# Linear attention and a gated mixing layer: two token tiles of batch 0 in plain float32, a second buffer for weight combinations, shorter roots

## The chip, the cores and the metric

One core of a Trainium2 chip runs the whole program. The metric is the device time of one execution in microseconds; a version's time is the median of its runs. TensorE multiplies matrices, VectorE, ScalarE (called ACT in the rows) and GpSimd (called POOL) do the elementwise work, and SyncE (SP) issues nearly all transfers. Each engine takes its instructions strictly in the order in which the program lists them, and waits on semaphores for what the others produce.

## The reference

Batch 4, 4 heads, 1088 tokens, head width 32 (together 128 columns), hidden width 1024.

```python
phi(x): a = S1 x; b = S2 x (8 numbers each); phi = outer(a, b)      # 64 features a token
kv = sum_s phi(k) v^T;  z = sum_s phi(k)
x  = phi(q) kv / (phi(q) z + 1e-6)                                   # heads side by side: x is [b, 1088, 128]
h  = gelu_tanh(x @ w_in);  u, v = halves of h                        # 512 columns each
v  = (v - mean(v)) / sqrt(var(v) + 1e-6) * g_ln                      # over the 512 columns
v_s[b, t, d] = sum_s w_sg[t, s] v[b, s, d] + b_sg[t]                 # mixing over the tokens
out = x + (u * v_s) @ w_out
```

`w_in`, `w_out`, S1 and S2 arrive as 64-bit floats and are taken apart on the chip; the rest is float32.

## The kernel before, in words

**Arithmetic.** A product of float32 operands is made of three products in the faster format `float32r`: each operand is rounded to a high word (a cast on ScalarE) and a remainder (the operand minus its high word, a subtraction on VectorE or GpSimd), and high x high, remainder x high and high x remainder are added up in PSUM. So the weights of the mixing stand in SBUF as `w_h` (high words, step `whi`, line 668) and `w_l` (remainders), and the normalised values as `ar` (both words). A few small products (features, attention) are plain float32 products; in the trace such a product stands as two records, a `float32r` product as one.

**Tiles.** The 1088 tokens are nine tiles of 128 (the last of 64). The mixing of one batch is cut into four blocks `db` of 128 hidden columns and, along the output tokens, three pieces `CH` of 420, 420 and 248. For batch 0, blocks 0 and 1 are made in the plain way: for each token tile t and piece, `z0` (block 0, line 690, into `po`) and the loop at line 1249 (block 1, into `pz` and one `ps` buffer) issue the high and remainder products of the values with `w_h` first, and the products with `w_l` later (`low`). All later batches use sums and differences of weight blocks, which save products.

**The start.** Batch 0's attention comes first: `first_loads` (line 434) brings S, k, q, v, `w_in` and the raw weight tiles `w_f` (544 KB each) in; `k1_0`, `features`, `k2_0` and `kv_0` make kv, `q2_0`, `qa`, `qp` and `q3_0` the numerator and denominator, `xd_0`, `xt_0`, `tr_0`, `x1` and `x2` make x (high `x_h`, low `x_l`), piece by piece (three pieces). Then, tile by tile, `v1_0` projects (three products), the gelu runs on ScalarE, VectorE takes mean and variance (`stats_0`, tiles 0 to 5) or ScalarE the sums (tiles 6 to 8), and the reciprocal root follows in groups of tiles, `GROUPS0` = (0,1), (2..5), (6..8): `Gate.first` makes the variance and a first guess from its bits (three small VectorE steps), `Gate.rest` (nine VectorE steps, group 0) or `Gate.rest_g` (11 or 12 GpSimd steps, groups 2 and 6) the root. A tile is scaled (`v3`, VectorE at line 666 or ScalarE at line 333), and `part` (line 670) makes its two words for the products.

**Remainders of the weights.** GpSimd makes them for tiles 0 to 6, three pieces each (`w_lo`, line 708, 21 steps), VectorE for tiles 7 and 8 (`late_low`, line 714). The pool `w` has ten buffers of a tile: nine raw tiles and one free; a remainder takes the buffer of the raw tile that the one before it has finished with, and the last buffer left becomes `t4a`. `HOLD` puts a copy into GpSimd's order so that a root is not delayed by remainders.

**Combinations.** `combine` (line 879) makes the sums and differences of the weight blocks for the later batches in eight rounds (four tile pairs, two halves of 210 columns). A round loads three pieces of the raw weights from DRAM into `tmp` (lines 891, 893), adds and subtracts on VectorE (lines 896 to 899), casts on ScalarE (lines 901, 902), makes remainders (903, 904) and stores high words and remainders to `td` in DRAM (line 906). All eight rounds use the one `tmp`: four parts for the sums and their remainders and three parts for the high words. `stream` brings the stored blocks back later. Beside it, `attention(1)` prepares batch 1 (k features at line 267, `q` products at line 976, its projections at lines 1037 to 1039, gelu 1046, squares 1049).

**The order of work.** A planner object only records steps with their dependencies; the order is written out by hand in `ORDER`, a list of all 1839 step numbers. A program walks it and issues each step on its engine, so each engine's queue is the list cut down to its steps. Some VectorE and GpSimd steps are marked `port`: a marked GpSimd step waits for the marked VectorE step listed before it.

Of the kernel before, what the change touches and what calls it, by code (L numbers as in the profile page):

```python
# [18 lines left out]
P = 128  # L19
# [13 lines left out]

LOWS = 7
ONA = ("wi1", "wi0", "wo")
HOLD = {12:0,15:2}
V30 = "VAVAVAAAA"
STAT = "VVA"
NORM = "VGG"
# [98 lines left out]
def f32(ap):  # L138
    return ap.bitcast(F32)
# [66 lines left out]
def tile_kernel(ctx: ExitStack, tc: tile.TileContext, qd, kd, vd, sd, wd, bd, wind, gd, woutd, identd, outd):  # L206
# [54 lines left out]
    for i in range(WARM):  # L261
        mm(pst[i % 3][:64, :64], lhsT=kp0[:, :64], rhs=kp0[:, :64], start=True, stop=True)

    def features(out, a, b):

        sh = [P, 2, 2, R, R]
        return V.tensor_tensor(  # L267
# [157 lines left out]
    for t in range(NT):  # L425
        w_f[t] = wpool([P, S], "w", f"w_f{t}")
# [952 lines left out]
```

## Time and profile before

| | |
|---|---|
| median of 3 runs | 323.56 us (322.67 to 324.0) |
| the profiled execution's own time | 325.58 us |
| its span, first to last instruction | 323.5 us |
| granted TensorE clock, mean | 0.999 of 2.4 GHz |
| busy: TensorE, VectorE, ScalarE, GpSimd | 310.4, 255.2, 206.7, 48.6 us |
| first mixing product | 33.09 us |

Times in the rows count from the first instruction. A row of an engine's order of time gives the start, the duration, the engine, the line, output and inputs, the shape and the count; brackets give the idle time before it and what ended it. Products overlap each other in the array, so a product lasts longer in its record than the step to the next one; the step is what it costs. The chain of waits is followed back from the last instruction: each piece is what the next one waited for.

### The profile page before, as it was taken

To read this page: it belongs to the slowest core of one execution; us is meant where nothing else is said; L and a number is where in the kernel's file an instruction comes from. 1 tells how busy PE (TensorE), PEld (TensorE's weight loads), DVE (VectorE), ACT (ScalarE), POOL (GpSimd) and SP (SyncE) were. 2 spreads that over 40 slices of the span, in tenths; PEclk is the share of its full clock that TensorE was granted. 3 is DMA by queue.
4 is the path that set the end of the run, shared out by engine and by line. 5 is a ranking of instruction groups with operands and counts; after the bars stand their busy time and mean duration, and the time that the engine had idled before them with its cause. 6 is when DMAs were issued, how large, how long until landed. Compare 5 with 4: busy or idle time off the path is not lost.

```text
span 323.5 us, 6439 instructions
## 1 busy us (share of the span) xinstructions
PE 310.4 (96%) x2318; PEld 282.2 (87%) x2318; DVE 255.2 (79%) x561; ACT 206.7 (64%) x491; POOL 48.6 (15%) x126
## 2 busy tenths in 40 slices
PE   7897999999998799999999999999999999999995
PEld 5565998998887798898899998988899999999995
DVE  4888989999957799987894497989874686878765
ACT  5589973738969886456877864528899933234321
POOL 0396791000003200000050200000006000000000
PEclk9999999999999999999999999999999999999999
DMA  6997775655876757678389047832173049005802
GB/s 203 369 305 265 238 199 175 201 164 158 249 209 191 203 173 220 146 247 239 98 261 321 6 131 246 265 88 63 28 266 135 1 113 305 34 21 165 283 6 69
DMA packets 42126, 57.08 MB, mean 176 GB/s; under 512 B 4080, under 2 KB 37104, under 8 KB 42096
## 3 DMA queue, kind: packets, MB, share of 16 engines
q1 hardware_dynamic: 41952, 56.64, 57.2%
q8 instruction: 18, 0.29, 0.4%
q14 instruction: 12, 0.10, 0.1%
q10 hardware_dynamic: 144, 0.05, 0.1%
HBM read 46.73 MB, written 9.95 MB: 175 GB/s over the span
## 4 chain that ended last, share of the span: by engine, by line
PE 70%; DMA 12%; DVE 7%; ACT 4%; SPq 3%; issue 2%; POOL 1%; DVEq 0%; ACTq 0%; POOLq 0%
PE pz L843 14%; PE pz L845 14%; PE pz L844 14%; DMA td<-tmp 3%; PE ps L758 2%; DMA tmp<-in_w 2%; PE ps L760 2%; PE ps L759 2%; PE pz L854 2%; DMA r<-in_q 2%; PE pz L855 2%; PE po L795 2%; DMA td<-w_l 2%; PE po L796 2%; PE po L797 2%
## 5 line engine op out<-in xcount | busy, mean ns | idle before, releaser
L843 PE MATMUL pz<-w_h,ar 128*128 128x420 f32 (+1 forms) x288 | 94.0, 327 | 0.0
L845 PE MATMUL pz<-w_l,ar 128*128 128x420 f32 (+1 forms) x288 | 93.1, 323 | 0.5 <-DMA w_l<-td 0.5
L844 PE MATMUL pz<-w_h,ar 128*128 128x420 f32 (+1 forms) x288 | 93.2, 324 | 0.0
L843 PEld LDWEIGHTS pz<-w_h,ar 128*128 128x128 f32 x288 | 54.1, 188 | 5.0 <-issue 1.8
L845 PEld LDWEIGHTS pz<-w_l,ar 128*128 128x128 f32 x288 | 54.2, 188 | 1.6 <-DMA w_l<-td 0.9
L844 PEld LDWEIGHTS pz<-w_h,ar 128*128 128x128 f32 x288 | 54.1, 188 | 1.0
L818 ACT CAST ar<-vn 128x512 fp32r<-128x512 f32 x40 | 24.7, 619 | 23.7 <-PE pz L845 18.2
L789 ACT CAST gh<-gt 128x420 fp32r<-128x420 f32 (+1 forms) x47 | 22.9, 493 | 24.1 <-DVE gt L788 22.1
L764 ACT ACTIVATE u<-ps 128x420 f32<-128x420 f32 (+1 forms) x48 | 22.0, 468 | 12.2 <-PE ps L760 10.7
L790 DVE TENSOR_TENSOR gl<-gt,gh 128x420 fp32r<-128x420 f32 (+1 forms) x47 | 24.9, 534 | 6.0 <-ACT gh L789 5.8
L819 DVE TENSOR_TENSOR ar<-vn,ar 128x512 fp32r<-128x512 f32 x40 | 27.1, 683 | 2.1 <-ACT ar L818 1.8
L333 ACT ACTIVATE vn<-vn,st 128x512 f32<-128x512 f32 x33 | 25.6, 812 | 0.9 <-POOL st L327 0.8
L788 DVE TENSOR_TENSOR gt<-gt,u 128x420 f32<-128x420 f32 (+1 forms) x47 | 24.8, 534 | 1.3 <-ACT u L764 0.4
L712 POOL TENSOR_TENSOR w_l<-w_f,w_h 128x420 fp32r<-128x420 f32 (+1 forms) x21 | 21.4, 1045 | 14.4 <-DVE sp_wi_t L492 12.7
L1049 ACT ACTIVATE kp<-vn,st 128x512 bf16<-128x512 f32 x27 | 19.4, 720 | 3.3 <-DVE vn L267 2.9
L774 DVE SCALAR_TENSOR_TENSOR gt<-pz,g_col,b_bc 128x420 f32<-128x420 f32 (+1 forms) x31 | 17.5, 571 | 3.9 <-PE pz L845 2.2
L1046 ACT ACTIVATE vn<-ps 128x512 f32<-128x512 f32 x27 | 16.0, 593 | 4.9 <-PE ps L1039 4.8
L316 POOL TENSOR_TENSOR st<-st 128x4 f32<-128x4 f32 (+2 forms) x8 | 2.1, 268 | 100.6 <-DVE st L298 100.6
L758 PE MATMUL ps<-x_h,win_h 128*128 128x420 f32 (+1 forms) x48 | 16.2, 337 | 0.1
L759 PE MATMUL ps<-x_h,win_l 128*128 128x420 f32 (+1 forms) x48 | 15.7, 328 | 0.0
L760 PE MATMUL ps<-x_l,win_h 128*128 128x420 f32 (+1 forms) x48 | 15.7, 327 | 0.0
L795 PE MATMUL po<-gh,wout_h 128*128 128x420 f32 (+1 forms) x47 | 15.7, 333 | 0.0
(260 smaller groups left out, 703.1 us busy)
## 6 DMA issues: line engine op xcount, KB each, us to landing
w_h<-td SPq DMA_DIRECT2D x26, 420.0 KB
w_l<-td SPq DMA_DIRECT2D x52, 210.0 KB
td<-tmp SPq DMA_DIRECT2D x16, 315.0 KB
w_f<-in_w SPq DMA_DIRECT2D x9, 544.0 KB
eb<-dq SPq DMA_DIRECT2D x6, 364.0 KB
ea<-dq SPq DMA_DIRECT2D x12, 182.0 KB
vn<-in_k SPq DMA_DIRECT2D x3, 576.0 KB
tmp<-in_w SPq DMA_DIRECT2D x8, 210.0 KB
```

The costliest lines, as they stand in the source:

```text
L333: return A.activation(self.vn(t), self.vn(t), AF.Identity, bias=self.nm[:, t : t + 1], scale=self.rs[:, t : t + 1])
L758: mm(o, lhsT=win_h[:, ws], rhs=xh[:, cs], start=True, stop=False)
L759: mm(o, lhsT=win_l[:, ws], rhs=xh[:, cs], start=False, stop=False)
L760: mm(o, lhsT=win_h[:, ws], rhs=xl[:, cs], start=False, stop=True)
L788: add("V", dv(cw), lambda: V.tensor_mul(gt(k)[:, :cw], gt(k)[:, :cw], utt[plan.got[u]][:, :cw]), r=[u], w=[k], free=[u], port=1)
L789: add("A", ac(cw), lambda: A.copy(ght[plan.got[h]][:, :cw], gt(k)[:, :cw]), r=[k], take={h: "gh"})
L790: add("V", dv(cw), lambda: V.tensor_sub(glt[plan.got[l]][:, :cw], gt(k)[:, :cw], f32(ght[plan.got[h]][:, :cw])), r=[h, k], take={l: "gl"}, ...
L818: add("A", ac(n), lambda: A.copy(dst[:, 0], q()), r=r, w=[key])
L819: add("V", dv(n), lambda: V.tensor_sub(dst[:, 1], q(), f32(dst[:, 0])), r=r, w=[key], port=1)
L843: mm(o, lhsT=ar[e][:, 0, t], rhs=wh, start=first, stop=False, skip_group_check=True)
L844: mm(o, lhsT=ar[e][:, 1, t], rhs=wh, start=False, stop=False, skip_group_check=True)
L845: mm(o, lhsT=ar[e][:, 0, t], rhs=wl, start=False, stop=last, skip_group_check=True)
```

## The change

- **`WHOLE = (0, 1)`**: in blocks 0 and 1 of batch 0, token tiles 0 and 1 are multiplied in one plain float32 product each, the scaled values `vn` with the raw weights `w_f`. Their `part` steps and their products with words are gone. Their remainders `w_l`, which later batches need, are made by VectorE after the last raw product (`late_low`, put behind `raws`); GpSimd makes all remainders of tiles 2 to 8. The pool's buffers are handed out in the order 2 to 8, 0, 1.
- **`tm2`**: the second half of each combination round has a buffer of its own for the four parts; the high words (`hi`) stay in the one `tmp`.
- **Roots**: `first` is two steps, not three; it runs on GpSimd wherever `rest_g` follows. `rest` is eight steps, not nine: a polynomial in place of two rounds of Newton's method.
- The split of S gives two of its eight steps to ScalarE; the split of `w_in`'s second half gives one subtraction (`l1`) to GpSimd. The switches `KG`, `QG` and `FILL` are empty or zero: their new branches run nothing.
- **`ORDER`** is a new list of 1816 steps. SyncE now loads: S, the large piece of k, the small piece of k, q's first third, v (two), `w_in`'s second half, q's other thirds, the identity, `w_f` 2, 3, a piece of batch 1's q, `w_f` 4, `w_in`'s first half, a piece of batch 1's q, the first pieces of `tmp`, batch 1's k, then `w_f` 0, 1, 8, 6, 5, 7. Before it was: S, the small piece of k, q's first third, `w_in`'s second half, the large piece of k, v's first part, q's second third, v's second part, `w_f` 0, the identity, q's last third, `w_f` 1, 2, 3, batch 1's k. VectorE's list now has, after the last statistics: the root of tiles 0 and 1, the scaling of tile 0, one combination step, and only then the first features of batch 1. TensorE's list has the projections in the tile order 2, 3, 4, 0, 5, 1, 6, 7, 8, then two q products and three k products of batch 1, then ten of the twelve raw products before the first product of tile 2's words; batch 1's key-value products come later. GpSimd's list has eight remainder pieces, then the roots of groups 2 and 6, then the other thirteen pieces.

```diff
+ROOT = (1.0, 0.99999624, 1.49998809, 2.51218104, 4.40140684)
+WHOLE = (0, 1)
 LOWS = 7
-ONA = ("wi1", "wi0", "wo")
-HOLD = {12:0,15:2}
+ONA = ("s", "wi1", "wi0", "wo")
+HOLD = {}
+LOWG = ("wi1",)
...
+    tm2 = const([P, 4 * HW], "tm2")
...
-        def first(self, t0, n, summed=True):
+        def first(self, t0, n, summed=True, by=None):
             ve, y = (x[:, :n] for x in self.ch[t0][:2])
...
-            V.tensor_scalar(yi, ve.bitcast(I32), 1, None, op0=ALU.logical_shift_right)
-            return V.tensor_scalar(yi, yi, -1.0, float(0x9EF759DF), op0=ALU.mult, op1=ALU.add)
+            return by.tensor_scalar(y.bitcast(I32), ve.bitcast(I32), -0.5, float(0x1EF759DF), op0=ALU.mult, op1=ALU.add)
...
             V.tensor_mul(h, y, y)
             V.tensor_mul(h, h, ve)
-            V.tensor_scalar(p, h, 1.5, 2.5, op0=ALU.mult, op1=ALU.add)
-            V.tensor_mul(p, p, h)
-            V.scalar_tensor_tensor(y, p, 1.875, y, op0=ALU.add, op1=ALU.mult)
-            V.tensor_mul(h, y, y)
-            V.tensor_mul(h, h, ve)
-            V.scalar_tensor_tensor(self.rs[:, ts], h, 1.5, y, op0=ALU.add, op1=ALU.mult)
+            V.tensor_scalar(h, h, 0.5, None, op0=ALU.add)
+            V.scalar_tensor_tensor(p, h, ROOT[3] / ROOT[4], h, op0=ALU.add, op1=ALU.mult)
+            for c in ROOT[2:0:-1]:
+                V.scalar_tensor_tensor(p, p, c / ROOT[4], h, op0=ALU.add, op1=ALU.mult)
+            V.scalar_tensor_tensor(self.rs[:, ts], p, ROOT[0] / ROOT[4], y, op0=ALU.add, op1=ALU.mult)
...
-    for t in range(NT):
+    turns = [t for t in range(NT) if t not in WHOLE] + list(WHOLE)
+    for t in turns:
         w_f[t] = wpool([P, S], "w", f"w_f{t}")
...
-        onA = n > 16 and name in ONA
+        onA = name in ONA
...
-            step(("first", t0), "V", 0.49, lambda t0=t0, n=n, s=summed: g.first(t0, n, s), bn, port=1)
-            step(("norm", t0), "G", 4.1, lambda t0=t0, n=n, s=summed: g.rest_g(t0, n, s), [("first", t0)])
+            step(("norm", t0), "G", 4.1, lambda t0=t0, n=n, s=summed: (g.first(t0, n, s, G), g.rest_g(t0, n, s))[1], bn)
...
+        if t in WHOLE:
+            mm(o, lhsT=vn[:, t, :P], rhs=w_f[t][:, c0 : c0 + cw], start=t == 0, stop=False, skip_group_check=True)
+            return
...
-                s = tmp[:, : 4 * HW].rearrange("p (a c) -> p a c", c=HW)
+                s = (tm2 if h else tmp)[:, : 4 * HW].rearrange("p (a c) -> p a c", c=HW)
                 hi = f32r(tmp[:, 4 * HW :].rearrange("p (a c) -> p a c", c=HW))
-                k = [("tmp", i) for i in range(4)]
+                k = [("tm2" if h else "tmp", i) for i in range(4)]
...
-            add("V", 0.55, lambda t0=t0, n=n: g.first(t0, n), r=mk, w=[nk], port=1)
-            add("G", 3.5, lambda t0=t0, n=n: g.rest_g(t0, n), r=mk, w=[nk])
+            add("G", 3.9, lambda t0=t0, n=n: (g.first(t0, n, by=G), g.rest_g(t0, n))[1], r=mk, w=[nk])
...
+                if t in WHOLE:
+                    mm(o, lhsT=vn[:, t, P : 2 * P], rhs=w_f[t][:, cs], start=t == 0, stop=False, skip_group_check=True)
+                    return
...
         if i == NT - 1:
+            for t in WHOLE:
+                lo = late_low(t, lo + raws)
             for x in range(NT):
-                for cj in range(3):
+                for cj in range(3 if x not in WHOLE else 0):
```

## Rows read from the trace of the kernel before

**Rows 1.** The page's parts 1 and 2: busy us by engine; traffic in 40 slices of 8.09 us.
```profile
PE 310.4 (96%) x2318; PEld 282.2 (87%) x2318; DVE 255.2 (79%) x561; ACT 206.7 (64%) x491; POOL 48.6 (15%) x126
...
GB/s 203 369 305 265 238 199 175 201 164 158 249 209 191 203 173 220 146 247 239 98 261 321 6 131 246 265 88 63 28 266 135 1 113 305 34 21 165 283 6 69
```

**Rows 2.** Stretches: us, busy us (count) of PE, PEld, DVE, ACT, POOL, clock, DMA share, GB/s.
```profile
27.88:33.09 5.21, 3.01 (x69) 2.60 (x68) 4.61 (x21) 5.11 (x20) 3.25 (x14) 1.00 0.64 214
...
94.00:110.00 16.00, 13.52 (x159) 11.85 (x158) 11.56 (x31) 12.84 (x37) 2.47 (x11) 1.00 0.71 216
...
160.00:314.20 154.20, 154.20 (x1052) 145.37 (x1051) 114.83 (x239) 90.92 (x214) 12.21 (x44) 1.00 0.47 146
```

**Rows 3.** TensorE in order of time: start, us, line, shape, count.
```profile
20.12 0.50 PE L633 MATMUL ps<-win_h,x_h 128*128 128x512 f32 x1
...
27.49 0.40 PE L635 MATMUL ps<-win_h,x_l 128*128 128x512 f32 x1
...
33.09 0.38 PE L697 MATMUL po<-w_h,ar 128*128 128x248 f32 x1
...
34.05 0.35 PE L697 MATMUL po<-w_h,ar 128*128 128x420 f32 x1
34.24 0.35 PE L699 MATMUL po<-w_h,ar 128*128 128x420 f32 x1
```

**Rows 4.** VectorE in order of time, 22 to 33 us.
```profile
22.07 0.70 DVE L639 BATCH_NORM_STATS2 st<-vn 128x6 f32<-128x512 f32 x1 [0.59 <-ACT vn L650]
...
28.63 0.17 DVE L296 TENSOR_SCALAR st<-st 128x2 f32<-128x2 f32 x1
...
31.00 1.09 DVE L267 TENSOR_TENSOR vn<-ps,kb 128x256 f32<-128x256 f32 x3
32.01 0.54 DVE L666 TENSOR_SCALAR vn<-vn,st 128x512 f32<-128x512 f32 x1
```

**Rows 5.** TensorE in order of time, its two waits between 94 and 110 us.
```profile
98.28 1.15 PE L941 MATMUL ps<-sk,vn 128*64 128x64 f32 x24 [0.81 <-ACT vn L1046]
...
108.55 0.53 PE L976 MATMUL ps<-qld,sk 128*64 128x180 f32 x4 [1.66 <-ACT u L764]
```

**Rows 6.** The chain of waits, 98 to 106 us: start, us, what.
```profile
98.52 2.70 DMA td<-tmp
101.24 4.08 DMA tmp<-in_w
```

**Rows 7.** ScalarE in order of time, the cast of line 901.
```profile
106.66 0.72 ACT L901 CAST tmp<-tmp 128x630 fp32r<-128x630 f32 x1 [1.56 <-DVE tmp L898]
```

**Rows 8.** The queue of SyncE, two of the first loads.
```profile
2.10 0.43 SPq L444 DMA_DIRECT2D sg_wraw_wi<-in_w_in  x1
2.58 0.43 SPq L437 DMA_DIRECT2D k<-in_k  x1
```

**Rows 9.** TensorE in order of time, 9 to 11.3 us.
```profile
9.04 0.92 PE L526 MATMUL ps<-sk,k 128*64 128x64 f32 x24 [1.48 <-DMA k<-in_k]
10.37 0.56 PE L604 MATMUL ps<-r,sg_sab 64*128 64x384 f32 x1 [0.41 <-DMA r<-in_q]
...
10.77 0.48 PE L604 MATMUL ps<-r,sg_sab 64*128 64x384 f32 x1
...
11.22 2.32 PE L534 MATMUL pz<-sg_vx,vn 128*64 128x64 f32 x72
```

**Rows 10.** The chain of waits, plain float32 products in batch 0 and at the end.
```profile
11.29 2.25 PE pz L534 x72
...
319.39 0.55 PE po L1200 x2
...
320.35 0.47 PE po L1200 x2
```

**Rows 11.** GpSimd's groups by line and shape: count, busy us, mean ns.
```profile
L712 POOL TENSOR_TENSOR w_l<-w_f,w_h 128x420 fp32r<-128x420 f32 x14 | 16.2, 1174 | 12.8 <-DVE sp_wi_t L492 12.7
L712 POOL TENSOR_TENSOR w_l<-w_f,w_h 128x248 fp32r<-128x248 f32 x7 | 5.5, 787 | 1.6 <-DVE st L298 1.6
```

More of the change, by code (lines that the diff above doesn't have):

```diff
@@ L262, in tile_kernel, with features @@
         mm(pst[i % 3][:64, :64], lhsT=kp0[:, :64], rhs=kp0[:, :64], start=True, stop=True)
[L264 removed]
+    def features(out, a, b, by=None):
         sh = [P, 2, 2, R, R]
[L267 removed]
+        return (by or V).tensor_tensor(
             out.rearrange("t (p h i j) -> t p h i j", p=2, h=2, i=R),
[L269 removed]
+            (a.rearrange("t (p h i) -> t p h i", p=2, h=2) if by else a[:, :64].rearrange("t (p x h i) -> t p x h i", p=2, x=2, h=2)[:, :, 0]).unsqueeze(4).broadcast_to(sh),
             b.rearrange("t (p h j) -> t p h j", p=2, h=2).unsqueeze(3).broadcast_to(sh),
@@ L666, in tile_kernel @@
                 step(("v3", t), "V", 0.45, lambda t=t: V.tensor_scalar(g.vn(t), g.vn(t), g.rs[:, t : t + 1], g.nm[:, t : t + 1], op0=ALU.mult, op1=ALU.add), [("norm", t0)], w=vk[t], port=1)
+    for i in range(FILL):
+        k = ("fill", i)
+        if i < FILL // 2:
+            step(k, "PE", 0.2, lambda k=k: (mm(ps(k)[:64, :64], lhsT=sk[:, :64], rhs=sk[:, :64], start=True, stop=True),
+                                            mm(ps(k)[:64, :64], lhsT=sk[:, :64], rhs=sk[:, :64], start=True, stop=True)), ["sk"], take={k: "ps"}, free=[k])
+        else:
+            step(k, "PE", 0.17, lambda k=k: mm(ps(k)[:, : 3 * P], lhsT=win_h[:, DG : DG + P], rhs=xh0[:, : 3 * P], start=True, stop=True), [("wi1", "hi")], r=[("x", 0, 0)], take={k: "ps"}, free=[k])
     for t in range(NT):
@@ L681, in tile_kernel @@
     for t0 in range(0, 8, 2):
-        part(0, t0, 2, 2 + t0 // 4, ("a0", t0))
+        n = 2 - sum(t in WHOLE for t in (t0, t0 + 1))
+        if n:
+            part(0, t0 + 2 - n, n, 2 + t0 // 4, ("a0", t0))
     last_part(0, 1)
     for e in range(2):
-        part(1, 4 * e, 4, e, ("ar", e))
+        n = 4 - sum(t // 4 == e for t in WHOLE)
+        part(1, 4 * e + 4 - n, n, e, ("ar", e))
     last_part(1, 0)
@@ L705, in tile_kernel, with remainder @@
         for ci in range(3):
+            if t in WHOLE:
+                step(("z0", t, ci), "PE", 4 * pe(CH[ci][1]), lambda t=t, ci=ci: z0(t, ci, False), [("v3", t), f"w{t}"], r=[("vn", 0, t, 0)], w=[("po", ci)])
+                continue
             step(("z0", t, ci), "PE", (2 if t < 8 else 1) * pe(CH[ci][1]), lambda t=t, ci=ci: z0(t, ci, False), r=zkeys(t) + [("w", t, ci, 0)], w=[("po", ci)])
-    def w_lo(t, c):
-        if c == 0:
+    def remainder(t, c, e):
+        if not c:
             w_l[t] = wpool([P, S], "w", f"w_l{t}", F32R)
-        cs = slice(CH[c][0], CH[c][0] + CH[c][1])
-        return G.tensor_sub(w_l[t][:, cs], w_f[t][:, cs], f32(w_h[:, t, cs]))
@@ L714, in late_low @@
-    def late_low(t):
-        w_l[t] = wpool([P, S], "w", f"w_l{t}", F32R)
+            if t == NT - 1:
+                e.memset(f32(w_l[t][64:128]), 0.0)
+        cs = slice(0, S) if c is None else slice(CH[c][0], CH[c][0] + CH[c][1])
         r = slice(0, P if t < NT - 1 else 64)
-        if t == NT - 1:
-            V.memset(f32(w_l[t][64:128]), 0.0)
-        return V.tensor_sub(w_l[t][r], w_f[t][r], f32(w_h[r, t]))
+        return e.tensor_sub(w_l[t][r, cs], w_f[t][r, cs], f32(w_h[r, t, cs]))
@@ L721, in tile_kernel, with late_low @@
     lo = []
-    for t in range(NT):
-        if t >= LOWS:
-            lo = [add("V", 1.2 + 1.0 * (t == NT - 1), lambda t=t: late_low(t), w=[("w", t, c, 1) for c in range(3)], r=[("w", t, c, 0) for c in range(3)], after=lo, port=1)]
+    def late_low(t, after):
+        return [add("V", 1.2 + 1.0 * (t == NT - 1), lambda: remainder(t, None, V), w=[("w", t, c, 1) for c in range(3)], r=[("w", t, c, 0) for c in range(3)], after=after, port=1)]
+    for t in turns[: NT - len(WHOLE)]:
+        if turns.index(t) >= LOWS:
+            lo = late_low(t, lo)
@@ L725, in tile_kernel @@
             continue
         for c in range(3):
-            if 3 * t + c in HOLD:
-                t0 = HOLD[3 * t + c]
-                lo.append(ids["norm", t0])
-                if plan.tasks[lo[-1]]["eng"] == "V":
-                    lo = [add("G", 0.2, lambda t0=t0: G.tensor_copy(pad, g.rs[:, t0 : t0 + 1]), after=lo)]
-            lo = [add("G", 0.92, lambda t=t, c=c: w_lo(t, c), w=[("w", t, c, 1)], r=[("w", t, c, 0)], after=lo, port=1)]
-    lo = lo[0]
-    done_lo = lo
+            lo = [add("G", 0.92 + (t == NT - 1 and not c), lambda t=t, c=c: remainder(t, c, G), w=[("w", t, c, 1)], r=[("w", t, c, 0)], after=lo, port=1)]
@@ L1248, in tile_kernel @@
     units = [(0, ci) for ci in range(3)]
+    raws = [ids["z0", t, ci] for t in WHOLE for ci in range(3)]
     for i in range(2 * NT):
```

45 lines of the change are left out of this document (33 added, 12 removed), and 183 rows, old and new, of the table ORDER.

## The prediction

> **What bounds the kernel now.** I read the busy shares first: TensorE is busy for 96% of the span [rows 1], so only its idle time and its amount of work can move the end. Next the busy times by stretch [rows 2]: from 160 to 314.2 us it is busy always. Two stretches hold holes that this change touches: 27.88 to 33.09 us (3.01 of 5.21 busy) and 94 to 110 us (13.52 of 16). VectorE is the next engine (4.61 of 5.21 us in the first hole), but behind a full TensorE its time costs nothing.
>
> Then TensorE's own order of time [rows 3]. Batch 0's value projections run from 20.12 to 27.49 us, small work of batch 1 follows, and the first mixing product starts at 33.09 us. Its first four products, of 248 columns, take until 34.05, 0.96 us, where 4 x 0.112 = 0.45 would do (products of 420 columns follow each other every 0.19 us: 0.452 ns a column). So the full stream begins, in effect, at 33.6 us. VectorE's order [rows 4] says why: statistics from 22.07, the root of tiles 0 and 1 in twelve small steps from 28.63 to 31.00, three features of batch 1 (1.01 us), the scaling of tile 0 at 32.01, and after that a cast and a subtraction before a product may start.
>
> The second hole is a transfer's. TensorE waits 0.81 us at 98.28 and 1.66 us at 108.55 [rows 5], and the chain leads back over ACT's cast of line 901 [rows 7] and VectorE to the load of `tmp` (101.24, 4.08 us) and to the store out of the same `tmp` (98.52, 2.70 us) that had to land first [rows 6]. ACT takes its instructions in order: the cast, late by 1.56 us, holds up the normalisation and the gelu behind it, and TensorE waits for that gelu.
>
> **The change, part by part** (against the profiled execution, 325.58 us with a span of 323.5; the median of the runs, 323.56, lies 2.02 us under its own time, and I carry the difference over to it).
>
> *Start of the mixing products.* Three things shorten the way. First, SyncE's list now loads both pieces of k before all else; before, the large piece went out behind the 512 KB of `w_in` [rows 8] and TensorE waited for it until 9.04 [rows 9]; raw weight tile 0 (544 KB), which went out ahead of the last third of q, now comes after batch 1's keys. In return q's second third stands behind v and `w_in`, 0.3 MB more: it let TensorE start at 10.37 [rows 9] and would, at 369 GB/s [rows 1], land 0.8 us later. Following the new lists with the old durations I reach the first projection at 18.5 instead of 20.12; the bounds are 0 and -1.6, I take -1.2, nearer the walk. Second, VectorE loses work on the way: three steps of the other group's root (0.6 us, to POOL), two of twelve steps (2.37 us becomes 1.97) and the three features (behind the scaling now). Statistics from 20.9, plus 28.63 - 22.07 - 0.6 = 5.96, plus 1.97, plus 0.54 for the scaling and 0.1 to hand over: 29.5 us. Third, a raw product reads the scaled tile itself, with no cast and no subtraction. 33.6 to 29.5 is **-4.1** (bounds -4.6, and -2.6 with no gain from the loads and some of the features still in front). The small products of batch 1 that stand before it (about 2.3 us) fit behind projections that end near 27. Those that multiply keys and values, a third of 72 records that took 2.25 us in batch 0 [rows 10], come after it now: **+0.75**.
>
> *The raw products.* Removed: three products a tile and half, 2 tiles x 2 halves x 1088 columns x 3 x 0.452 ns = 5.9 us. Added: the same columns in plain float32, which no row shows at this shape; plain float32 stands as two records a product. Three rows bound it. The query products (384 columns, 64 rows deep, two side by side) step every 0.42 us from 10.37 to 11.22 [rows 9]: 2.2 ns a column for both records, 9.6 us in all, +3.7, the upper end. The last products of the kernel, two records each, take 0.55 us at 160 columns and 0.47 at 88 [rows 10]: 0.08 us for 72 columns, 1.1 ns a column, 4.8 us in all, -1.1, the lower end; it rests on one difference of modelled ends. Batch 0's key-value products, 128 rows deep as the raw ones, take 2.25 us for 72 records of 64 columns, two side by side [rows 10]: 62.5 ns a pair, 1.95 ns a column, 8.5 us. I take this row, a run of products back to back like the raw ones: **+2.6**.
> The Trainium skill ("FP8 and Floating Point Precision", TensorE Precision Notes) says that true float32 makes four passes through the array; at 0.452 ns a column that would be 7.9 us, the term +2.0 and the sum 0.6 us lower. The row taken lies above it, the last products far below.
>
> *Two buffers for the combinations* (`tm2`). Loads of the second half no longer wait until the first half's store has read its buffer. The two waits are worth 0.81 + 1.66 = 2.47 us [rows 5]; bounds 0 and -2.5, since the rounded words still share one buffer. A load of 4.08 us started one round earlier covers a store of 2.70 [rows 6], so I take most: **-2.3**.
>
> *Fewer steps for the roots, first steps on POOL, split of S.* Ten VectorE steps instead of twelve are counted above. In the later batches VectorE loses three steps a group and POOL gains two; TensorE is full there [rows 2], so nothing is gained; uncovered, two small steps would cost 0.6 us a group. In the split of S two of eight steps of 16 columns go to ACT, beside the others: 0, at most 0.3 either way.
>
> *The weights' remainders.* POOL now makes all 21 pieces for tiles 2 to 8 and takes the first steps of two roots and one subtraction of the split of `w_in`; VectorE makes tiles 0 and 1 late, after the raw products (it must: the raw tiles stay in use until then). TensorE covers this: raw products 8.5 us, first products of tiles 2 to 8 12.7 us, other work about 3 us, and the remainders of tiles 2 to 6 4.9 us feed it until about 58.5. POOL's work is 14 x 1.17 + 7 x 0.79 for the pieces [rows 11], some 4 for the splits' three steps at that rate, some 8 for the roots and 1 for a fill, 35 us from about 13.5: done near 49, some waiting included near 50. Price 0, cover 8 us.
>
> *The new order.* All steps are listed anew, and every list leaves some holes: the old one leaves 2.5 us between 94 and 110 us [rows 2]. For new ones **+0.5** (0 to +2).
>
> Sum: -4.1 + 0.75 + 2.6 - 2.3 + 0.5 = -2.55: 323.0 for the profiled execution, **321.0 us** at the median.
>
> **The rivals.**
> - *Raw products at the pace of the query products*, +3.7 instead of +2.6: 322.1, and up to 322.5 with a gap at each change of kind. For it: the nearest count of columns. Against: that row works on half the depth, in pairs.
> - *The combinations still wait.* ACT's cast writes rounded words that the previous store must have read, one buffer for both halves. If that store, not the load, is the late one, the holes stay: 321.0 + 2.3 = 323.3. Against: store and load together took 6.8 us, the store alone 2.70 [rows 6].
> - *Raw weights late.* Tiles 0 and 1 end 6.7 MB of loads. The first three slices move 7.1 MB in 24.3 us [rows 1], so they land near 25; only later than 29.5 do they cost, and 3 us more give 324. Little for it.
> - *Slower: POOL becomes the bound.* The place is the last remainders (tiles 7 and 8), at the end of batch 0's first two halves. Done at 50 as planned they cost nothing; POOL decides from 58.5 on, and 62.5 or later gives 325.0 or more. Against: that is a third more than its whole work. The Trainium skill (GPSIMD Engine Reference, Key points) says that POOL shares its SBUF interfaces with VectorE and contends with instructions of two inputs; no row here separates the two cases.
> - *It does not start earlier*: the loads give nothing and features and ACT's steps crowd before the raw products: with -2.6 for the first term, 322.5.
>
> **How the numbers follow.** The forecast, 319 to 321.9, holds 0.55; the raw pace 0.13 (half of it under 321.9); combinations 0.10; late weights 0.03; no earlier start 0.06; POOL or another new wait 0.08; and 0.05 for better than 319, with raw products near their lower end. A measurement here tells 0.5%, 1.6 us, from no change. Faster by more than that (under 321.9): 0.55 + 0.05 + 0.06 = 0.66; within: 0.07 + 0.10 + 0.03 + 0.06 = 0.26; slower 0.08. The range: below, first term and combinations at their best and a quarter of the way to the cheap raw products, -4.6 + 0.75 + 1.7 - 2.5 + 0 = -4.65, gives 318.9, and 317.8 takes in some of the better case; above, 323.6, where the combinations' rival ends.
>
> **What the changed profile would show.** First mixing product at 29.5 us instead of 33.09, raw products from `w_f` and `vn` without a hole behind them; two records a product, 8.5 us in all. No wait of over 0.5 us before TensorE between 90 and 112 us, and no idle ACT before line 901's cast. POOL's last remainder near 50 us. TensorE's idle time down by 5 to 6 us. Wrong would be: a first product after 31 us, raw products above 9.6 us, holes near 60 us that end on a remainder of POOL, or the two holes again, ended by a store of `tmp`.

## The result, and the profile after

The change is **faster** by 1.2%: 319.58 us median of 4 runs (319.47 to 319.6) against 323.3 for the kernel before on the same chip, a ratio of 0.9877 with a 95% interval of 0.9859 to 0.9895. The profiled execution took 319.47 us with a span of 317.7; in the profile that the prediction was read from they were 325.58 and 323.5. The forecast was 321.0 in a range of 317.8 to 323.6: side and range were right, the saving at the median was 3.7 us where 2.55 had been worked out, and several terms behind the sum were wrong in size.

The page of the changed kernel, busy us by engine, beside [rows 1]:

```profile
PE 309.9 (98%) x2306; PEld 282.4 (89%) x2306; DVE 251.5 (79%) x530; ACT 207.2 (65%) x492; POOL 55.8 (18%) x143
```

TensorE's busy time is almost that of before (310.4); it is idle for 7.8 us of the span instead of 13.1. GpSimd's work has grown from 48.6 to 55.8 us.

The stretches that [rows 2] showed, here for the changed kernel (us, then busy us and count of PE, PEld, DVE, ACT, POOL, then granted clock, DMA share, GB/s). The first is the one between the last projection and the first mixing product:

```profile
25.93:30.04 4.11, 2.47 (x45) 1.78 (x44) 3.66 (x17) 3.22 (x12) 2.82 (x13) 1.00 0.01 2
94.00:110.00 16.00, 16.00 (x187) 14.89 (x182) 12.06 (x30) 15.87 (x44) 7.05 (x26) 1.00 0.77 230
160.00:308.40 148.40, 148.18 (x1002) 141.15 (x1001) 108.43 (x217) 87.88 (x205) 10.68 (x39) 1.00 0.46 139
```

From 94 to 110 us TensorE is busy all the time (13.52 of 16 before). The first stretch has shrunk from 5.21 to 4.11 us, but 1.6 us of it are still idle.

TensorE in order of time, beside [rows 3, 9]:

```profile
4.44 2.19 PE L532 MATMUL ps<-sk,k 128*64 128x64 f32 x36 [0.26 <-DMA k<-in_k]
...
8.28 2.30 PE L540 MATMUL pz<-sg_vx,vn 128*64 128x64 f32 x64
...
18.64 0.50 PE L651 MATMUL ps<-win_h,x_h 128*128 128x512 f32 x1
...
27.11 0.57 PE L967 MATMUL ps<-sk,vn 128*64 128x64 f32 x12 [0.65 <-ACT vn L668]
28.60 0.53 PE L1002 MATMUL ps<-qld,sk 128*64 128x182 f32 x4 [0.93 <-ACT vn L668]
28.96 1.15 PE L967 MATMUL ps<-sk,vn 128*64 128x64 f32 x24
30.04 0.97 PE L1284 MATMUL pz<-w_f,vn 128*128 128x420 f32 x2
...
39.34 0.46 PE L729 MATMUL po<-w_h,ar 128*128 128x420 f32 x1 [0.42 <-DVE ar L698]
```

Both pieces of k are there at 4.44: all 36 feature products run in one go, and none waits for k at 9 us any more. The first projection starts at 18.64 (20.12 before), the first raw product (L1284, `w_f` and `vn`) at 30.04 (33.09 before). In front of it stand batch 1's k products (L967) and q products (L1002), which waited 0.65 and 0.93 us for ScalarE (L668, the last gelus).

VectorE in order of time, beside [rows 4]:

```profile
20.74 0.69 DVE L657 BATCH_NORM_STATS2 st<-vn 128x6 f32<-128x512 f32 x1 [0.60 <-ACT vn L668]
...
26.32 0.17 DVE L303 TENSOR_SCALAR st<-st 128x2 f32<-128x2 f32 x1
...
28.30 0.55 DVE L683 TENSOR_SCALAR vn<-vn,st 128x512 f32<-128x512 f32 x1
```

The statistics start at 20.74, the root of tiles 0 and 1 at 26.32, and the scaled tile 0 is ready at 28.85: 1.2 us before the product that reads it starts. So VectorE, which set the start before, no longer does.

The four longest entries of TensorE's waits in the changed kernel (total, times, longest):

```profile
PE ps L269 <- POOL kp L267: 0.9, 1, 0.9
PE ps L1002 <- ACT vn L668: 0.9, 1, 0.9
PE pz L618 <- DVE r L604: 0.7, 1, 0.7
PE ps L967 <- ACT vn L668: 0.6, 1, 0.6
```

None of them is a transfer of `tmp` or the cast behind one [rows 5 to 7]. The last remainders on GpSimd's own list, beside [rows 11]:

```profile
51.98 3.46 POOL L748 TENSOR_TENSOR w_l<-w_f,w_h 64x420 fp32r<-64x420 f32 x3
```

They end at 55.4 us, later than the 50 I had worked out; no product waits for them. SyncE's issues, beside [rows 8]:

```profile
1.18 0.42 SPq L443 DMA_DIRECT2D k<-in_k  x1
...
17.33 0.33 SPq L435 DMA_DIRECT2D w_f<-in_w  x1
29.17 0.33 SPq L997 DMA_DIRECT2D qld<-in_q  x1
```

The large piece of k (L443) goes out second, at 1.18 us (it was behind `w_in`). The rows also show a trait of the new list that mattered in the experiments: after 17.33 nothing is issued until 29.17 (the stretch from 25.93 to 30.04 above moves 2 GB/s). SyncE issues its transfers in the order of its list and stands at a load of batch 1's q (line 997), whose buffer is still to be read by the q product at 28.60.

### The profile page after: what moved, and what is told of

It reads as the page before. It is cut to its first block, busy times and chain, and to the rows that moved or that the text cites. A ratio compares the mean times of both kernels' runs of the same rounds, so it can differ in the third digit from the quotient of the medians.

```text
span 317.7 us, 6381 instructions
## 1 busy us (share of the span) xinstructions
PE 309.9 (98%) x2306; PEld 282.4 (89%) x2306; DVE 251.5 (79%) x530; ACT 207.2 (65%) x492; POOL 55.8 (18%) x143
## 4 chain that ended last, share of the span: by engine, by line
PE 82%; DVE 6%; ACT 5%; DMA 2%; issue 1%; SPq 1%; POOL 1%; POOLq 0%; DVEq 0%; ACTq 0%
PE pz L869 15%; PE pz L871 14%; PE pz L870 14%; PE ps L784 2%; PE po L821 2%; PE po L823 2%; PE ps L785 2%; PE ps L786 2%; PE ps L1029 2%; PE po L822 2%; PE ps L1063 2%; DMA r<-in_q 2%; PE ps L540 2%; PE ps L1065 2%; PE ps L1064 2%; PE pz L880 2%
## 5 line engine op out<-in xcount | busy, mean ns | idle before, releaser
L748 POOL TENSOR_TENSOR w_l<-w_f,w_h 128x420 fp32r<-128x420 f32 (+3 forms) x21 | 21.7, 1061 | 2.6 <-POOL w_l L748 1.0
L301 POOL TENSOR_SCALAR st<-st 128x5 f32<-128x5 f32 (+2 forms) x7 | 1.4, 197 | 89.1 <-ACT kp L1075 87.4
```

## The experiments

Every ratio is against the kernel before on the same chip, in runs taken beside those of the version.

**1. How much do two executions of one program differ?** Both kernels once more, unchanged, for a second profile of each.

> The kernel of before, unchanged, for a second profiled execution. The one read for the prediction took 325.58 us, 2.3 above the median of its runs. If those 2.3 us are waits that most executions do not have: own time near 323.3, and TensorE's waits (10.8 us in the first profile, 1.5 of them on k at 9.04 us and 2.5 at the combinations) shorter by about 2 us. If they lie outside the waits: the same waits, and a time near 323.3 all the same.

> The changed kernel, unchanged, beside the others of this call, so that a few tenths can be told: 319.6 us, TensorE's waits before 30 us about 3.7 us as in its first profile.

Measured: 323.75 us (ratio 1.0008, 0.9984 to 1.0032) and 319.62 us (0.9876, 0.9843 to 0.991). The spans of the two profiled executions were 321.3 and 317.1 (321.26 and 317.14). The second profile of the kernel before has a smaller hole than [rows 2]:

```profile
94.00:110.00 16.00, 15.12 (x167) 13.43 (x167) 12.06 (x33) 14.48 (x40) 3.54 (x16) 1.00 0.74 227
```

TensorE in order of time, the one wait that is left there:

```profile
106.92 0.53 PE L976 MATMUL ps<-qld,sk 128*64 128x180 f32 x4 [0.81 <-ACT u L764]
```

0.88 us idle, not 2.48. The first wait of [rows 5], ahead of L941, is absent, and the second, ahead of L976, has shrunk from 1.66 to 0.81 us. The holes change from one execution to the next, and the execution that the prediction was read from was a long one, 2.02 us above the median. That bears on the term for `tm2`.

For a comparison of like with like I use this second pair of profiles below. Their spans differ by 4.1 us: the first mixing product starts 3.6 us earlier, and 0.5 us are gained behind it. The first mixing product of the kernel before, then that of the changed kernel:

```profile
33.10 0.38 PE L697 MATMUL po<-w_h,ar 128*128 128x248 f32 x1
```

```profile
29.49 0.97 PE L1284 MATMUL pz<-w_f,vn 128*128 128x420 f32 x2
```

**2. The raw products by themselves.** Every raw product issued twice, to add their time once more.

```diff
-            mm(o, lhsT=vn[:, t, :P], rhs=w_f[t][:, c0 : c0 + cw], start=t == 0, ...)
+            for r in range(2):
+                mm(o, lhsT=vn[:, t, :P], rhs=w_f[t][:, c0 : c0 + cw], start=t + r == 0, ...)
```

> The changed kernel with each of the twelve raw products issued twice (the second adds the same product again, so the sums of tiles 0 and 1 are doubled). 4352 columns more on a TensorE that has no idle time behind them. At 1.95 ns a column, the price taken in the prediction: +8.5, 328.1. At 1.70 ns, the step from the first raw product (30.04) to the first word product that follows at full pace (36.81, less 0.19) over 3856 columns: +7.4, 327.0. At 1.1 ns, the lower bound: +4.8, 324.4. Less than the price by up to 0.4 us if the wait of 0.42 us at 39.34 us goes into the longer time.

Measured: 325.9 us (1.0093, 1.006 to 1.0126), span 324.0, so +6.3 us. TensorE in order of time (a row's shape is that of its first record; the row at 38.22 holds eight records of 248 columns and then four of 420):

```profile
29.66 1.68 PE L1286 MATMUL pz<-w_f,vn 128*128 128x420 f32 x4
31.17 4.39 PE L722 MATMUL po<-w_f,vn 128*128 128x420 f32 x12
35.40 2.98 PE L1286 MATMUL pz<-w_f,vn 128*128 128x420 f32 x8
38.22 3.25 PE L722 MATMUL po<-w_f,vn 128*128 128x248 f32 x12
41.30 1.57 PE L1286 MATMUL pz<-w_f,vn 128*128 128x420 f32 x4
```

From 31.17 to 38.22 there are 20 records of 420 columns (12 of L722 and 8 of L1286), 0.3525 us each; the next 12, four of 420 columns and eight of 248, take 3.08 us until 41.30, which leaves 0.2085 for a record of 248 (3.08 less four times 0.3525, divided by eight). A product is two records: 0.705 us for 420 columns, or 1.68 ns a column. All 4352 columns cost 7.31 us (eight products of 0.705 and four of 0.417), neither the 8.5 that I took nor the 9.6 of the rival. Of the 7.31 us added here, 0.42 fall into the wait that the changed kernel has at 39.34, and the first raw product started 0.38 us earlier, which leaves 6.5 against 6.3 measured.

The three word products that each one replaces step at 0.19 us for 420 columns [rows 3], 5.9 us for all, as the prediction has it. So plain float32 costs +1.4 us, or about 0.13 us for a product of 420 columns, half of the +2.6 predicted.

The Trainium skill ("FP8 and Floating Point Precision", TensorE Precision Notes) counts four passes through the array for a true float32 product. The trace agrees: at the granted clock of 1.00, 2.4 GHz, the step of 0.705 us is 1692 cycles, four for each of the 420 columns and 12 more.

**3. Is VectorE still what the first raw product waits for?** The root of tiles 0 and 1 made twice, which puts 1.9 us more on VectorE in front of the scaling.

```diff
-... (g.first(t0, n, s), g.rest(t0, n, s)), bn, port=1)
+... (g.first(t0, n, s), g.rest(t0, n, s), g.first(t0, n, s), g.rest(t0, n, s)), bn, port=1)
```

> The changed kernel with the root of tiles 0 and 1 computed twice on VectorE: ten small steps more, 1.98 us, ahead of the scaling. If VectorE's path sets the start, as the prediction's sum has it: +2.0, 321.6. If TensorE's own list, busy with the products that stand ahead until 30.04 us where the scaling ends at 28.85, leaves 1.1 us of room: +0.9, 320.5. If the start does not hang on VectorE at all: 319.6.

Measured: 320.46 us (0.991, 0.9882 to 0.9938), +0.9 us. TensorE in order of time:

```profile
17.83 0.50 PE L651 MATMUL ps<-win_h,x_h 128*128 128x512 f32 x1
...
29.98 1.77 PE L1284 MATMUL pz<-w_f,vn 128*128 128x420 f32 x2 [0.63 <-DVE vn L683]
```

From the first projection to the first raw product it is 12.15 us here, 11.40 in the changed kernel (18.64 to 30.04): 1.9 us of added VectorE work moved the product by 0.75, and it now waits for the scaling (L683). About 1.1 us of room lay behind VectorE: TensorE's own list (q and k products and their waits for ScalarE) sets the start.

This profiled execution was the longest of its six (322.03 us), and the stretches show one reason:

```profile
28.00:29.10 1.10, 1.04 (x28) 0.89 (x24) 0.93 (x6) 0.74 (x3) 0.29 (x2) 0.99 0.00 0
29.10:35.90 6.80, 6.17 (x17) 3.08 (x12) 6.62 (x18) 6.51 (x16) 4.50 (x13) 0.50 0.97 333
35.90:38.00 2.10, 2.10 (x9) 1.39 (x8) 2.07 (x3) 2.10 (x4) 1.24 (x3) 1.00 0.99 347
```

The granted clock was at 0.50 of 2.4 GHz, the level of 1.2 GHz, from 29.1 to 35.9 us. It fell after waits of 0.64 and 0.93 us, and before the wait for the scaling. The changed kernel has the first two waits too (0.65 and 0.93) and stayed at 1.00 in both its profiles, so the added root is not shown to be what made the clock fall. The median of the six mixes executions with and without such a fall: three with a mean clock of 0.998 took 319.98 to 320.18 us. The 0.75 us do not rest on the clock: the raw product follows the scaling, which VectorE ends at 29.93 us.

The changed kernel itself does not always keep the clock up. Of its ten recorded executions four have a mean granted clock of 0.999 or 1.000 and took 318.88 to 319.57 us, the two profiled ones among them. The six others have 0.994 or 0.995, an estimated 3 us at 0.50 (0.005 of 318 us, at half), and took 319.43 to 321.69. No profile shows where.

**4. The two buffers.** Undone in the changed kernel, where `ORDER` moves the loads of the second halves, and the steps that hang on them, behind the stores; then added alone to the kernel before, with each second half's loads moved one round earlier.

```diff
-                s = (tm2 if h else tmp)[:, : 4 * HW].rearrange("p (a c) -> p a c", c=HW)
+                s = tmp[:, : 4 * HW].rearrange("p (a c) -> p a c", c=HW)
...
-                k = [("tm2" if h else "tmp", i) for i in range(4)]
+                k = [("tmp", i) for i in range(4)]
```

> The changed kernel (319.58 us) with both halves of a combination round in one buffer again; the list of steps is the same but for the loads of the second half, which move behind the stores that they now wait for. If the second buffer removed the two waits of 0.81 and 1.66 us, they come back in some form between 80 and 110 us: +2.3 us, 321.9. If the new order, or the work taken from VectorE, removed them: no wait of TensorE over 0.5 us there, under 320.1.

Measured: 359.16 us (1.111, 1.1063 to 1.1156), far off what either theory gave. TensorE's two longest groups of waits:

```profile
PE pz L869 <- DVE gt L800: 8.7, 3, 8.3
PE pz L869 <- ACT ar L844: 6.9, 1, 6.9
```

The longest stretch at a low clock:

```profile
70.20:80.50 10.30, 5.01 (x15) 4.78 (x16) 6.69 (x15) 2.92 (x7) 0.00 (x0) 0.50 0.41 130
```

With one buffer a load has to stand behind a store of the round before, and the list was written for two: the load holds SyncE, all later loads stand behind it, and ScalarE and VectorE then hold their queues. Around these waits the granted clock stood at 0.50 for 38 us in five stretches, in which TensorE worked for 27 us, so at most some 13 of the 40 us lost are the clock's (an estimate: half of that work). That is the price of a list that doesn't fit its buffers, not of the buffer, so the run does not measure the term. The other direction does:

```diff
+    tm2 = const([P, 4 * HW], "tm2")
...
-                s = tmp[:, : 4 * HW].rearrange("p (a c) -> p a c", c=HW)
+                s = (tm2 if h else tmp)[:, : 4 * HW].rearrange("p (a c) -> p a c", c=HW)
...
-                k = [("tmp", i) for i in range(4)]
+                k = [("tm2" if h else "tmp", i) for i in range(4)]
```

> The kernel of before (323.3 us) with a second buffer for the combinations and nothing else; the loads of a round stand one round earlier in SyncE's list. If the late loads made the two waits at 98.28 and 108.55 us, both go: -2.3, 321.0. If the rounded words, which still share one buffer, hold the rounds up: 323.3, waits as before. In between: one of the two goes, 322.5 (the first) or 321.7 (the second).

Measured: 322.62 us (0.9976, 0.9956 to 0.9996), -0.7 us at the median. The stretch that has the holes:

```profile
94.00:110.00 16.00, 16.00 (x176) 14.62 (x175) 11.60 (x31) 15.75 (x43) 5.36 (x22) 1.00 0.75 228
```

No idle time is left in it. The shared rounded words, which the second rival feared, hold up no product there. So the mechanism is as predicted, and its size at the median is 0.7 us, near the 0.88 us of idle time that the second profile of before has in that stretch.

**5. The order of the loads.** First the changed kernel with its ten first loads in the old order.

```diff
-    1, 11, 12, 13, 15, 3, 2, 4, 14, 16, 17, 18, 47, 42, 43, 45, 46, 49, 5, 61,
+    1, 11, 12, 13, 15, 2, 4, 10, 14, 16, 17, 18, 47, 42, 43, 45, 46, 49, 3, 53,
...
```

> The changed kernel with the first ten loads in the order of before (S, small piece of k, q's first third, w_in's second half, large piece of k, v's first part, q's second third, v's second part, identity, q's last third), and the first k products, their copies and features in the order that goes with it. If k ahead of w_in is what brings the first projection from 20.12 to 18.64 us, it comes at about 19.9 and the rest follows: +1.2, 320.8. If the same bytes decide whatever their order: within 0.3 of the unchanged kernel, 319.6.

Measured: 324.25 us (1.002, 1.0002 to 1.0039), +4.6 us where about 1 was expected. TensorE in order of time, then two stretches:

```profile
8.81 0.91 PE L532 MATMUL ps<-sk,k 128*64 128x64 f32 x12 [1.91 <-DMA k<-in_k]
...
12.57 3.40 PE L540 MATMUL pz<-sg_vx,vn 128*64 128x64 f32 x64
...
23.81 0.50 PE L651 MATMUL ps<-win_h,x_h 128*128 128x512 f32 x1
```

```profile
6.90:8.81 1.91, 0.00 (x1) 0.00 (x1) 0.00 (x0) 0.00 (x0) 0.00 (x0) 0.98 0.95 343
8.81:15.30 6.49, 6.49 (x80) 5.14 (x82) 3.29 (x9) 2.04 (x6) 0.00 (x0) 0.50 1.01 347
```

TensorE waited 1.91 us for the large piece of k, as the kernel before does for 1.48 [rows 9], but behind that wait the granted clock was 0.50 for 6.49 us, and the first 64 records of the key-value products took 3.40 us instead of 2.30. The first projection came at 23.81 instead of 18.10 to 18.64. To take the clock out, the same order with 16 small products (32 records, their result unread) in that wait:

```diff
-            step(("q2_0", c, i), "PE", 1.3, lambda c=c, i=i: q2_0(c, i), ...)
+            step(("q2_0", c, i), "PE", 1.3, lambda c=c, i=i: (q2_0(c, i), [mm(pst[2][:64, :64], lhsT=kp0[:, :64], rhs=kp0[:, :64], start=True, stop=True) for r in range(16 if c + i == 0 else 0)])[0], ...)
```

> The kernel old_loads (324.25 us) with sixteen products of 64 columns more, that nothing reads, issued while TensorE waits for the large piece of k, where its profile shows 1.9 us of idle time and then a granted clock of 0.50 from 8.8 to 15.3 us. If the low clock is most of what old_loads lost: the clock stays at 1.00 and the time falls by about 3 us, to 321.0, with 1.2 us left for the later k. If the order of the loads itself cost the 4.6 us: 324.2 as before.

Measured: 323.46 us (0.9996, 0.9973 to 1.002). Two stretches:

```profile
8.70:15.30 6.60, 6.59 (x113) 4.59 (x113) 4.66 (x11) 2.92 (x8) 0.00 (x0) 1.00 1.02 341
...
34.00:36.00 2.00, 2.00 (x5) 0.93 (x4) 0.83 (x3) 2.00 (x4) 1.53 (x6) 0.51 0.94 346
```

The clock is at 1.00 through the first stretch and the first projection comes at 21.45, 2.4 us earlier than without the extra products, by doing more work. That the half clock made those 2.4 us is shown. But only 0.8 us arrived at the end, and in this profile the clock falls to 0.51 later, at the raw products (32.5 to 36.0), behind the same two waits of 0.63 and 0.93 us that the changed kernel has. Three of its executions kept a mean clock of 1.000 and took 322.20 to 322.64 us: with the clock up the old order still costs 2.6 to 3.0 us. Nor is the clock all of what `old_loads` lost: two of its executions at 1.000 took 325.25 and 325.40 us, the nine at 0.988 to 0.995 took 323.76 to 325.21. The remaining delay of the first projection, 21.45 against 18.10 to 18.64, comes with the order of the loads and of the first k steps that go with it.

The other direction, the new order of the first loads alone in the kernel before:

```diff
-    1, 11, 12, 13, 14, 15, 16, 17, 18, 42, 43, 2, 0, 4, 52, 53, 46, 10, 3, 5,
+    1, 3, 2, 4, 5, 6, 10, 7, 8, 9, 29, 11, 12, 13, 14, 15, 16, 17, 18, 42,
...
```

> The kernel of before (323.5 us in the last call) with one part of the change alone: the first ten loads in the new order, both pieces of k ahead of everything but S, and the first k products, copies and features in the order that goes with it. As the prediction has it, the first projection comes 1.2 us earlier (18.9 instead of 20.12) and all behind it: 322.3. If the wait for k was a full 1.5 us in every execution and the clock of TensorE stays up: 322.0. If the order of the loads gives nothing: 323.5.

Measured: 327.81 us (1.0129, 1.0097 to 1.0161), slower by 4.2. The longest of TensorE's waits, then one stretch:

```profile
PE ps L604 <- DVE sp_wi_t L470: 2.1, 1, 2.1
```

```profile
14.00:16.00 2.00, 2.00 (x43) 2.00 (x42) 1.82 (x4) 0.83 (x3) 0.04 (x1) 0.50 0.97 393
```

`w_in` now lands later, and VectorE's list still has the splitting of `w_in` (L470) ahead of what TensorE needs: 2.1 us of waiting, one more wait of 1.4, then half clock (12.7 to 16.1 us; all six executions have a mean clock of 0.983 to 0.995). So neither direction gives the price of the loads by itself. Each undoes a fit between loads, VectorE's list and TensorE's list; that the new loads pay only with the new lists fits both runs, but no run shows what they pay there.

**6. Can the room behind VectorE be used?** If TensorE's list sets the start, projecting tiles 0 and 1 first and putting raw products ahead of the k products should start them earlier. Three versions of the changed kernel, each a reordering of `ORDER` alone. In the first, the tiles go 0, 1, 2, ... and their root comes right behind their statistics.

```diff
-    170, 28, 133, 101, 136, 134, 137, 226, 110, 139, 227, 140, 111, 112, 135, 124, 138, 44, 142, 113,
+    170, 28, 124, 101, 127, 125, 128, 226, 110, 133, 227, 134, 111, 112, 126, 136, 129, 113, 130, 131,
...
```

> The changed kernel with tiles 0 and 1 projected first instead of fourth and sixth; VectorE makes their root and scales tile 0 right after the third piece of x, and only then takes the statistics of tiles 2 to 5; four raw products stand ahead of the first k products of batch 1. The raw weights 0 and 1 were loaded long before 30 us. If TensorE's 1.6 us of idle time between 26 and 30 us come from the late projection of tiles 0 and 1: the first raw product at 26.3 us instead of 30.04 and -1.2, 318.4. If the root of tiles 2 to 5 on POOL, which then starts near 28.3 instead of 25.2, becomes the late one: an idle TensorE before the first word product near 35 us instead, and 319.6, or up to 1 us more.

Measured: 321.77 us (0.9938, 0.9918 to 0.9958), slower than the change by 2.1 us. The raw products started at 25.65, but GpSimd paid for it:

```profile
24.65 3.46 POOL L748 TENSOR_TENSOR w_l<-w_f,w_h 128x248 fp32r<-128x248 f32 x4 [6.01 <-DVE vn L683]
```

Its remainder pieces, listed behind the scaling and marked `port`, waited 6.01 us for it, the other tiles' root came late behind them, and TensorE waited 1.37 us until 36.96 for tile 2's words. In the second, more pieces stand ahead of the root.

```diff
-    125, 228, 229, 40, 127, 143, 150, 128, 151, 230, 231, 141, 412, 369, 248, 144, 528, 154, 152, 129,
+    170, 28, 124, 101, 127, 125, 128, 226, 110, 133, 227, 134, 111, 112, 126, 136, 129, 113, 228, 229,
+    230, 231, 369, 248, 232, 233, 130, 131, 44, 139, 137, 40, 142, 140, 150, 143, 151, 135, 412, 138,
...
```

> The kernel root_first with what delayed the root of tiles 2 to 5 put right: POOL's first eight pieces are listed ahead of the scaling of tile 0 (they had waited for it until 24.65 us), and ScalarE's gelu of tile 8 ahead of the copy of the k products (it had waited 2.18 us behind it). If those two made root_first slow: the root of tiles 2 to 5 done near 32 us instead of 35.1, the first word product near 35 us, and 318.4, 1.2 under the changed kernel. If VectorE and ScalarE, full in this stretch, are the bound behind it: the first word product at 36.8 as in the changed kernel, and 319.6.

Measured: 320.72 us (0.9917, 0.9893 to 0.994), 1.1 us above the change. VectorE, then GpSimd, then TensorE in order of time:

```profile
22.75 1.01 DVE L304 TENSOR_SCALAR st<-st 128x2 int32<-128x2 int32 x1
23.79 1.01 DVE L309 TENSOR_TENSOR st<-st 128x2 f32<-128x2 f32 x1
```

```profile
22.63 2.16 POOL L748 TENSOR_TENSOR w_l<-w_f,w_h 128x420 fp32r<-128x420 f32 x2
```

```profile
26.82 0.97 PE L1284 MATMUL pz<-w_f,vn 128*128 128x420 f32 x2 [0.67 <-DVE vn L683]
...
40.02 0.46 PE L729 MATMUL po<-w_h,ar 128*128 128x420 f32 x1 [1.22 <-DVE ar L698]
```

Two small steps took 1.01 us each, where the same steps take 0.17 and 0.16 in the changed kernel: they end at 23.76 and 24.80, and GpSimd's two pieces, back to back from 22.63, take 1.08 us each and end at 24.79. The first raw product waits for it (26.82), and tile 4's words are late by 1.22 us. The Trainium skill (GPSIMD Engine Reference, Key points) says that GpSimd shares its SBUF interfaces with VectorE and contends with its two-input instructions and with those in a 2-port mode. The rows agree for L309, which reads two inputs; L304 reads one, and no row shows whether it is in such a mode. In the third version, where no remainder piece runs beside them, the two steps take 0.17 and 0.16 us again.

In the third, some of those pieces stand later again, and some of the splitting of `w_in` later.

```diff
-    125, 228, 229, 40, 127, 143, 150, 128, 151, 230, 231, 141, 412, 369, 248, 144, 528, 154, 152, 129,
+    230, 369, 248, 130, 131, 44, 139, 137, 40, 142, 140, 150, 143, 151, 135, 231, 232, 412, 138, 528,
...
```

> The kernel root_first2 with two more moves, after its profile: no piece of a remainder on POOL beside VectorE's root of tiles 0 and 1 (two of its small steps took 1.01 us each instead of 0.17), and the split of w_in's first half, 3.6 us of VectorE in the profile of the changed kernel, behind the words of tiles 2 to 5 instead of ahead of them; the first two k products of batch 1 and their features move into VectorE's wait for POOL's root. If those steps were what kept the words late in root_first2: root of tiles 2 to 5 near 32 us, the first word product near 35 us with no wait of over 0.3 us ahead of it, and 318.6, 1.0 under the changed kernel. If VectorE and POOL, whose work is the same and full until 56 us, only give it back later (a remainder or a feature late between 42 and 60 us): 319.6 to 320.5.

Measured: 323.28 us, on a chip where the kernel before took 325.38 (0.9933, 0.9906 to 0.9959). TensorE in order of time:

```profile
25.83 0.97 PE L1284 MATMUL pz<-w_f,vn 128*128 128x420 f32 x2
...
39.30 0.46 PE L727 MATMUL po<-w_h,ar 128*128 128x420 f32 x1 [1.25 <-ACT w_h L692]
...
44.76 0.34 PE L540 MATMUL ps<-ea,vn 128*64 128x64 f32 x4 [2.90 <-issue]
```

The first raw product starts at 25.83, 3.7 to 4.2 us before that of the changed kernel, and TensorE has no wait from there until 38 us. Then come 1.25 us for the high words of a raw weight tile that is loaded late (SyncE's queue, which stood from 18.2 to 31.5), and 2.90 us for the features behind the moved splitting. Together 4.15 us: what was won is given back. And behind the second wait the clock fell once more:

```profile
45.10:48.50 3.40, 3.40 (x64) 3.39 (x61) 2.92 (x4) 3.40 (x8) 3.27 (x3) 0.50 0.68 218
```

The two of its six executions with a mean clock of 0.999 took 322.15 and 322.46 us, the four at 0.994 and 0.995 took 323.26 to 323.66. So an earlier start is possible, and the next limits are SyncE's list, the features and the clock. None of the three beats the change; a version that also mends those two waits was not run.

## Why the prediction was right, and where it was wrong

The measured terms, from the second pair of profiles (321.26 and 317.14), counting TensorE from one product's start to the next with the idle time apart. The 0.45 us that the first four word products of before took too long (0.11 of it idle) stand in the first row, as in the prediction, and in no other:

| term | predicted | measured |
|---|---|---|
| start of the mixing products, from 33.6 | -4.1 | -4.06 (33.10 + 0.45 to 29.49) |
| key-value products of batch 1 behind it | +0.75 | +0.51 |
| raw products against the words' products | +2.6 | +1.54 (raw 6.73 and words 21.20, against words 26.39) |
| idle time: two buffers -2.3, holes of the new order +0.5 | -1.8 | -0.56 |
| q products -0.51, all others -1.05 | 0 | -1.56 |
| sum | -2.55 | -4.13 |

In the first pair (323.5 and 317.7), whose first member the prediction read, the same terms are -3.5, +0.5, +1.5, -2.7 and -1.7, -5.8 in all.

- **Start: right in size, by another way.** The chain through VectorE was read well, and was even faster than worked out (scaled tile at 28.85, not 29.4). I had let TensorE's small products "fit behind projections that end near 27"; they did not. They end at 30.04, held up by their waits for ScalarE. The first pair of profiles gives -3.5, the second, whose first projection came at 18.10, -4.1. The first projection gained 1.5 to 2.0 us where I took 1.2 for the loads. That size and range were met although the path was another is in part luck.
- **Raw products: the mis-sized term.** The step that failed is "I take this row, a run of products back to back like the raw ones": products of 64 columns, two side by side, at 1.95 ns a column. The raw products step at 1.68. By steps the term is +1.4, and with all products of the two blocks counted from start to start +1.5. Neither bound was reached, and the four passes (+2.0), which I had set aside for the row, were nearer.
- **Two buffers: right mechanism, read from one execution.** "The two waits are worth 0.81 + 1.66" priced an execution 2.02 us above the median and carried the result over to the median. In that execution the idle time did go, 2.7 us in the first pair. The second profile of before has one wait of the two, of 0.81 us, and alone the part gave -0.7. At the median the term was some 1.5 us too good; the sum still fell short of the gain, because raw products came out 1.1 us cheaper than worked out and the q products and small steps 1.6, which the sum does not have at all. That errors of both signs met in the forecast is luck too.
- **New order +0.5: held.** Its one new hole inside the mixing is the 0.42 us at 39.34.
- **Roots, split of S: 0, no run speaks against it,** and none undoes them alone. In the later batches TensorE is busy for 148.18 of 148.40 us. **Remainders: 0, right for the reason given**, but with less cover than the 8 us named. GpSimd ends at 55.44, and that last piece, of tile 8, is first read at 61.75. The closest is tile 7's second piece, which ends at 50.01 and is read at 52.28, where the prediction lets GpSimd decide only from 58.5 on.
- **Rivals.** Raw products at the query products' pace: refuted by experiment 2. Combinations still waiting: refuted by experiment 4 and by the full stretch from 94 to 110 us. Raw weights late: tiles 0 and 1 are not what the first raw product waits for. GpSimd as the bound: no product waits for a remainder. No earlier start: refuted. None named what the runs showed as a danger to this start, the clock falling behind a wait.

What stays open: the share of the loads, of the lists and of the raw products' shorter way (no cast, no subtraction) in the earlier start, which no run takes apart; and the -1.56 us. Of these, 0.5 are batch 1's q products, which step faster in their new place for a reason that no run isolates, 0.2 are the later batches' projections, and the rest is spread over more than a thousand products.

## What to carry to other kernels

Read a hole in at least two executions before pricing it, and price it against the median. When a critical engine is relieved, check the next engine's own list up to the same instruction: here 1.1 us of VectorE's gain ended behind small products that had been idle filling before. In a kernel whose order is written out by hand, loads, buffers and lists are one design; undoing one of them alone measures a mismatch (some 40 us for a buffer), not its worth. And read the mean clock of every execution beside its time: two executions of one list can differ by a stretch at half clock.

## What the runs showed of the hardware

- Behind waits of TensorE the granted clock fell to 0.50: for 6.5 us behind one of 1.91 us (experiment 5, old order), for 3.4 us behind one of 2.90 (experiment 6, third version). Behind two waits of about 0.6 and 0.9 us it fell for 6.8 us in experiment 3 and for 3.5 in experiment 5, and did not fall in the two profiles of the changed kernel: the same waits can go either way.
- Keeping TensorE busy with unread products through the wait of 1.91 us held the clock at 1.00 there and brought the first projection 2.4 us forward; 0.8 us of that arrived at the end.
- Plain float32 products of 128 x 128 by 420 columns step at 1.68 ns a column in two records of 0.3525 us, with nothing lost between one product and the next.
- Two VectorE steps on 2 elements a partition took 1.01 us each beside GpSimd's subtraction, and 0.16 to 0.17 without it; statistics beside the same work kept their 0.66 to 0.69 us.
